# Attention in pairs of blocks from the eleventh on, and gate weights in fewer visits, in a kernel that fuses attention with two expert layers on one core

## The chip, the cores and the metric

The kernel runs on one core of a Trainium2 chip. The core has five engines, each with its own instruction stream that it follows in order: TensorE (PE in the rows; PEld is its loading of weights), VectorE (DVE), ScalarE (ACT), GpSimd (POOL) and SyncE (SP), which here issues DMA transfers. They meet at semaphores: an instruction that needs another engine's result waits at the head of its own stream, and whatever stands behind it waits too. The metric is the device time of one execution in microseconds.

## What is computed

```python
def _attn_ref(q, k, v):            # q, k, v: 4 batches, 8 heads, 576 positions, 64 values
    scores = scale * np.matmul(q, k.transpose(0, 1, 3, 2))
    ...                            # heads 0-3: a band of 32 keys; heads 4-7: 32 keys, four apart
    scores = np.where(masks[None], scores, -1000000000.0)
    scores = scores - np.max(scores, axis=-1, keepdims=True)
    attn = np.exp(scores)
    attn = attn / (np.sum(attn, axis=-1, keepdims=True) + 1e-09)
    return np.matmul(attn, v)

def _moe_ref(x, w1, w2, w3, w_out):  # x: 2304 tokens of 512; w1, w2: 512 x 1024; w3: 1024 x 1024
    a = x @ w1
    b = x @ w2
    h = a * b @ w3
    return h @ w_out

def _moe2_ref(x, w_gate, w1, w2):    # 8 experts, 288 tokens each, chosen by the gate's logits
    logits = x @ w_gate
    ...                              # tokens go to experts in the order of their logits
    out[mask] = np.maximum(x[mask] @ w1[e], 0.0) @ w2[e]
```

## The kernel before

**Attention** (L166 to L277) works on 36 blocks: 4 batches, each of 9 blocks of 64 query positions for all 8 heads; a key block has 96 keys. In each batch the ninth block (j = 8) holds what is left over, and its matmuls are cut into halves. A block goes through these steps: QK on TensorE (`att_qk`, L166, into two banks of PSUM); mask and row maximum on VectorE (`att_max`, L185); exponentials on ScalarE (`att_exp`, L197); the reciprocal of the sums on VectorE and the product of probabilities with it on GpSimd (`att_norm`, L203, L207); transposes on TensorE and a copy of them to SBUF on ScalarE (`att_tr`, L209, L213, L215); probabilities times V on TensorE (`att_av`, L217, L226 and L229); and the result's high half by a copy on ScalarE (L249, L250), its low half by a subtraction on VectorE (`att_out`, L232, L251, L252). PSUM has eight banks: four with the tag "ab", two "h", one "tr", one "rt". QK uses "h" from block 7 on, transposes "tr", V "rt".

`attention` (L254) is a generator that software-pipelines these: with each block t it issues QK of t, then, after a `yield`, the output of t - 4, the maximum of t and the norm of t - 1; after another `yield`, exponentials of t, transposes of t - 2 and V of t - 3; then QK of t + 1 follows in the same step. A step is what runs between two yields; a block has two steps. Each block so has **one visit** to TensorE: transposes of one block, V of another, QK of a third.

**The first expert layer** (`moe`, L397) multiplies x by w1 and w2 and the two results with each other. fp32 values are split into a high and a low part, so each product takes three matmuls (L433 to L435). `moe(b)` yields before every six matmuls of 512 columns (or twelve of 256); I call what stands between two of its yields a **portion**. Batch 0 has 32 portions: 16 on halves of 256 tokens, 16 on 512. Batches 1 and 2 have 32 too. Batch 3 has 48, 16 of them on all batches' ninth blocks. The accumulators are "ab" banks, taken out by a copy on ScalarE (L438) and a product on VectorE (L440) one portion later.

**The order** of everything is that in which the program text runs; no scheduler moves it. The main loop (L492 to L520) walks over the portions, and ahead of each runs steps of attention while `steps < done * ATT_RATE + ...` (L507; 0.65 steps per portion, and 0.7 more for each of batch 0's first eight), or for as long as the batch's input isn't ready: a portion of `moe(b)` must come behind the outputs of batch b that it reads, and a loop at a batch's end runs attention until these are issued. Ahead of each portion of batches 0 and 1 also runs one step of narrowing: weights come as 64-bit numbers and are turned into fp32 by three instructions on VectorE (L135, L137, L139), then split on ScalarE and GpSimd (L121, L124) in batch 0, or written back to DRAM (L314).

**The gates** (`gates`, L332): the second layer's gate is multiplied through w_out and w3 while batch 3's portions run. From its fourth portion on, each portion is preceded by one step: eight times transposes of a piece of w_out (`turn`, L341) and a product with the gate (`gate`, L352, L355), where each step has the product of one piece and the transposes of the next; then w3 in two groups of four (L369 to L378), where a step holds two of eight parts k (L376, 16 passes), and between the groups six portions pass while the second group is fetched.

Of the kernel before, what the change touches and what calls it, by code (L numbers as in the profile page):

```python
# [9 lines left out]
F32 = mybir.dt.float32  # L10
# [25 lines left out]
START, ATT_RATE, LATE, EARLY, FIRST = 8, 0.65, 3, 7, 0.7  # L36
# [51 lines left out]
def body(tc, qk_d, v_d, ke_d, ve_d, msk_d, cst_d, tri_d, w1_d, w2_d, w3_d, wo_d, wg_d, e1_d, e2_d, out):  # L88
# [12 lines left out]
    pa = pool("pa")  # L101
# [45 lines left out]
    QK, KE, SC, V, VE, P, OT, AV, X = {}, {}, {}, {}, {}, {}, {}, {}, {}  # L147
# [18 lines left out]
    def att_qk(t):  # L166
# [4 lines left out]
        s = SC[t] = [bank([128, 2, KB], "h" if t >= EARLY else "ab") for _ in range(2)]  # L171
# [13 lines left out]
    def att_max(t):  # L185
# [3 lines left out]
        p = pa.tile([128, 4, KB], F32, tag="p", name="p", bufs=3)  # L189
        sm = pa.tile([128, 4, 4], F32, tag="sm", name="sm", bufs=3)  # L190
# [18 lines left out]
    def att_tr(t):  # L209
        p = P.pop(t)[0]  # L210
        o = bank([KB, 4, 128], "tr" if t >= EARLY else "h")
        for i in range(4):
            nc.tensor.transpose(o[:, i, :], p[:, i, :], ident)  # L213
        pt = OT[t] = pa.tile([KB, 4, 128], F32, tag="pt", name="pt", bufs=2)
        act(pt, o, AF.Copy)  # L215

    def att_av(t):  # L217
        pt, v, ve = OT.pop(t), V.pop(t), VE.pop(t, None)
        o = AV[t] = bank([128, 4, QB], "rt")
# [34 lines left out]
    def attention():  # L254

        for t in range(NT + 4):
            if t < NT:
                att_qk(t)
            if t + 3 < NT:
                qk_load(t + 3)  # L260
            yield t - 4
            if t >= 4:
                att_out(t - 4)
            if t < NT:
                att_max(t)
            if 1 <= t <= NT:
                att_norm(t - 1)
            yield t - 3
            if t < NT:
                att_exp(t)  # L270
            if 2 <= t < NT + 2:
                att_tr(t - 2)
            if 3 <= t < NT + 3:
                att_av(t - 3)
            if t + 1 < NT:
                v_load(t + 1)

# [56 lines left out]
    def gates():  # L334
# [6 lines left out]
        def turn(r):  # L341
            g, i = divmod(r, 4)
            t = bank([128, 4, 128], "tr")
# [4 lines left out]
            wt = p3.tile([128, 4, 128], F32, tag="wt", name="wt", bufs=1)  # L348
# [8 lines left out]
        for r in range(8):  # L357
            wt = turn(r)
            yield
            gate(r, wt)  # L360
        ts = p3.tile([128, 4, 128], F32, tag="ts", name="ts", bufs=1)[:, :2]
# [10 lines left out]
        for a, ms in enumerate(((4, 5, 6, 7), (0, 1, 2, 3))):  # L372
            ws = [narrowed["w3", m] for m in ms]
            for k in range(8):
# [3 lines left out]
                if k % 2:  # L378
                    yield
# [4 lines left out]
        wt = p3.tile([128, 4, 128], F32, tag="wt", name="wt", bufs=1)[:, :2]  # L384
# [789 lines left out]
```

## Time and profile before

| | |
|---|---|
| time of three runs, us | 741.73 (median), 739.2, 743.91 |
| time of the profiled execution, us | 737.08 |
| its span, first to last instruction, us | 735.3 |
| TensorE busy, us (share) | 706.5 (96%) |
| weight loads busy | 609.8 (83%) |
| VectorE busy | 411.8 (56%) |
| ScalarE busy | 353.5 (48%) |
| GpSimd busy | 262.2 (36%) |
| granted TensorE clock, mean | 0.998 of 2.4 GHz |

Attention and the first layer's batches 0 to 2 fill the span to about 225 us, batch 3 with the gates to about 300 us; then come the product of w3 and w_out, the routing and the eight experts. A busy share of TensorE is made of overlapping matmuls whose ends are modelled, so the distance from one start to the next tells more than the duration. In the rows of the timeline the columns are start, duration, engine, line, operation, output from inputs, shape and how many instructions the row merges.

### The profile page before, as it was taken

The numbers are of one execution on the slowest core, as the hardware profiler recorded it, in microseconds if no ns is written. First come the engines' busy times: TensorE is split into PE (matmuls) and PEld (weight loads), VectorE is DVE, ScalarE is ACT, GpSimd is POOL, SyncE is SP. The second block draws the span as 40 slices with busy tenths as digits, with TensorE's granted clock in tenths as the row PEclk, the third lists the DMA queues.
The fourth block names the chain that finished last, engine by engine and source line by source line (L and its number), as shares of the span: only waits on it lengthen the run. The fifth ranks groups of instructions, "written<-read, shape, count | busy, mean of one in ns | idle before, by whom it ended". The sixth has DMA issues, their size and how long they took to land.

```text
span 735.3 us, 16004 instructions
## 1 busy us (share of the span) xinstructions
PE 706.5 (96%) x6081; PEld 609.8 (83%) x6081; DVE 411.8 (56%) x1414; ACT 353.5 (48%) x812; POOL 262.2 (36%) x305
## 2 busy tenths in 40 slices
PE   4799999999999999999999999999999999999996
PEld 3589787787788878687877877789999999999995
DVE  3879887863321001167876677678777863234321
ACT  4676555455422222243445375436556656665432
POOL 1758522121100033633355453331314144754521
PEclk9999999999999999999999999999999999999999
DMA  8984899862023030110699999869898798995311
GB/s 298 341 267 142 299 300 328 284 235 75 29 85 145 2 115 1 49 45 30 115 133 131 175 150 221 139 206 229 201 268 219 194 259 234 267 317 172 126 33 33
DMA packets 59452, 126.66 MB, mean 172 GB/s; under 512 B 13680, under 2 KB 29168, under 8 KB 56816
## 3 DMA queue, kind: packets, MB, share of 16 engines
q1 hardware_dynamic: 27088, 89.46, 36.8%
q0 software_dynamic: 29696, 31.46, 25.6%
q10 hardware_dynamic: 2592, 4.72, 1.9%
q8 instruction: 48, 0.79, 0.5%
q14 instruction: 28, 0.23, 0.1%
HBM read 87.87 MB, written 15.73 MB: 141 GB/s over the span
## 4 chain that ended last, share of the span: by engine, by line
PE 77%; issue 6%; DVE 5%; ACT 4%; DMA 3%; POOL 3%; SPq 1%; POOLq 0%; ACTq 0%; DVEq 0%
PE ps_ab L433 10%; PE ps_ab L435 9%; PE ps_ab L434 9%; PE ps_ab L578 4%; PE ps_h L999 4%; PE ps_h L1000 3%; PE ps_h L1001 3%; PE ps_ab L1023 3%; PE ps_ab L580 3%; PE ps_ab L579 3%; PE ps_ab L1024 3%; PE ps_ab L1025 3%; PE ps_rt L226 2%; PE ps_rt L776 2%; PE ps_ab L547 2%
## 5 line engine op out<-in xcount | busy, mean ns | idle before, releaser
L207 POOL TENSOR_TENSOR p<-p,sm 128x384 f32<-128x384 f32 x36 | 41.6, 1157 | 125.9 <-ACT p L200 68.3
L1023 PE MATMUL ps_ab<-hh,w 128*128 128x288 f32 x248 | 75.8, 306 | 0.0
L1025 PE MATMUL ps_ab<-hh,w 128*128 128x288 f32 x248 | 73.1, 295 | 0.0
L1024 PE MATMUL ps_ab<-hl,w 128*128 128x288 f32 x248 | 73.0, 294 | 0.0
L463 POOL DMA_DIRECT2D wbl<-g x36 | 48.4, 1675 | 62.8 <-ACT wbl L461 53.8
L1011 ACT ACTIVATE hh<-ps_h 128x288 fp32r<-128x288 f32 x62 | 25.5, 412 | 87.6 <-PE ps_h L1001 87.5
L200 ACT ACTIVATE p<-p,sm 128x96 f32<-128x96 f32 x144 | 52.1, 363 | 28.4 <-DVE sm L193 28.3
L1012 DVE SCALAR_TENSOR_TENSOR hl<-ps_h,hh 128x288 fp32r<-128x288 f32 x62 | 28.2, 455 | 66.3 <-ACT hh L1011 66.2
L438 ACT ACTIVATE a<-ps_ab 128x512 f32<-128x512 f32 (+1 forms) x44 | 22.8, 519 | 84.9 <-PE ps_ab L435 75.3
L578 PE MATMUL ps_ab<-Wx,wbh 128*128 128x512 f32 x144 | 59.7, 415 | 0.0
L579 PE MATMUL ps_ab<-Wx,wbh 128*128 128x512 f32 x144 | 56.3, 391 | 0.0
L580 PE MATMUL ps_ab<-Wx,wbl 128*128 128x512 f32 x144 | 56.2, 390 | 0.0
L433 PE MATMUL ps_ab<-x,wah 128*128 128x512 f32 (+1 forms) x144 | 55.9, 388 | 0.0
L440 DVE TENSOR_TENSOR g<-a,ps_ab 128x512 f32<-128x512 f32 (+1 forms) x36 | 22.4, 622 | 58.4 <-PE ps_ab L435 58.4
L433 PE MATMUL ps_ab<-x,wbh 128*128 128x512 f32 (+1 forms) x144 | 54.5, 379 | 0.0
L434 PE MATMUL ps_ab<-x,wah 128*128 128x512 f32 (+1 forms) x144 | 53.4, 371 | 0.0
L435 PE MATMUL ps_ab<-x,wal 128*128 128x512 f32 (+1 forms) x144 | 53.4, 371 | 0.0
L435 PE MATMUL ps_ab<-x,wbl 128*128 128x512 f32 (+1 forms) x144 | 52.8, 367 | 0.0
L434 PE MATMUL ps_ab<-x,wbh 128*128 128x512 f32 (+1 forms) x144 | 52.7, 366 | 0.0
L1024 PEld LDWEIGHTS ps_ab<-hl,w 128*128 128x128 f32 x248 | 46.7, 188 | 0.1
L1023 PEld LDWEIGHTS ps_ab<-hh,w 128*128 128x128 f32 x248 | 46.8, 189 | 0.0
L1025 PEld LDWEIGHTS ps_ab<-hh,w 128*128 128x128 f32 x248 | 46.5, 188 | 0.0
(293 smaller groups left out, 2052.9 us busy)
## 6 DMA issues: line engine op xcount, KB each, us to landing
est<-e_dram SPq DMA_DIRECT2D x53, 512.0 KB, 5.4
w<-w_dram SPq DMA_DIRECT2D x16, 1024.0 KB, 9.3
qk<-qk_dram SPq DMA_DIRECT2D x36, 320.0 KB, 5.3
w<-est POOLq DMA_DIRECT2D x20, 512.0 KB, 7.0
wbl<-g POOLq DMA_DIRECT2D x28, 256.0 KB, 6.3
v<-v_dram SPq DMA_DIRECT2D x36, 192.0 KB, 4.3
kept<-f SPq DMA_DIRECT2D x12, 512.0 KB, 4.9
rows<-e_dram SPq DMA_DIRECT2D x11, 512.0 KB, 6.3
```

The lines of the kernel that those rows point to most:

```text
L200: act(p[:, i, :], p[:, i, :], AF.Exp, bias=sm[:, 1, i:i + 1], scale=-1.0, accum_out=sm[:, 2, i:i + 1])
L207: nc.gpsimd.tensor_tensor(p, p, sm[:, 3, :, None].to_broadcast([128, 4, KB]), op=OP.mult)
L433: mm(a, wh[:, k, fs], xh[:, k, ts], start=(k == 0), stop=False)
L434: mm(a, wh[:, k, fs], xl[:, k, ts], start=False, stop=False)
L435: mm(a, wl[:, k, fs], xh[:, k, ts], start=False, stop=(k == 3))
L463: nc.gpsimd.dma_start(x, src, accum_op=OP.add)
L578: mm(a, h[:, f, :], wh, start=(f == 0), stop=False)
L579: mm(a, h[:, f, :], wl, start=False, stop=False)
L580: mm(a, l[:, f, :], wh, start=False, stop=(f == 7))
L1023: mm(y, wh[:, f % 2, ds_], h, start=(f == 0), stop=False)
L1024: mm(y, wh[:, f % 2, ds_], l, start=False, stop=False)
L1025: mm(y, wl[:, f % 2, ds_], h, start=False, stop=(f == end))
```

## The change

Up to block 9 attention runs as before. From block 10 on (`ALONE`) it goes two blocks at a time, in four steps per pair, and each stage has a visit to itself per pair: V of the pair `turned` (both into one "rt" bank), transposes of the pair `ready` (one into "tr", one into an "ab" bank), QK of the pair `new` (both into the two "h" banks), all in one step; then the copies of the transposes and the outputs of `turned`; then the first maximum and both norms of `scored`; then the second maximum and both exponentials. A pair's QK is so three visits ahead of its V. The probability buffers become four, and the rate of steps in batch 0 is 0.72 (`RUSH`) in place of 0.65. In the gates, two pieces of w_out are turned per two steps, in "h" banks and with two buffers, and w3 takes one step per group of four.

```diff
-START, ATT_RATE, LATE, EARLY, FIRST = 8, 0.65, 3, 7, 0.7
+START, ATT_RATE, RUSH, LATE, EARLY, FIRST, ALONE = 8, 0.65, 0.72, 3, 7, 0.7, 10
...
     ident = C[:, C_ID:C_ID + 128]
-    QK, KE, SC, V, VE, P, OT, AV, X = {}, {}, {}, {}, {}, {}, {}, {}, {}
+    QK, KE, SC, V, VE, P, TR, OT, AV, X = {}, {}, {}, {}, {}, {}, {}, {}, {}, {}
...
-    def att_qk(t):
+    def att_qk(t, s=None):
         x = QK.pop(t)
-        s = SC[t] = [bank([128, 2, KB], "h" if t >= EARLY else "ab") for _ in range(2)]
+        s = SC[t] = s or [bank([128, 2, KB], "h" if t >= EARLY else "ab") for _ in range(2)]
         ke = KE.pop(t, None)
...
         m = 2 if j == 8 else int(j < 4)
-        p = pa.tile([128, 4, KB], F32, tag="p", name="p", bufs=3)
-        sm = pa.tile([128, 4, 4], F32, tag="sm", name="sm", bufs=3)
+        p = pa.tile([128, 4, KB], F32, tag="p", name="p", bufs=4)
+        sm = pa.tile([128, 4, 4], F32, tag="sm", name="sm", bufs=4)
         for i in range(4):
...
-    def att_tr(t):
+    def att_tr(t, tag):
         p = P.pop(t)[0]
-        o = bank([KB, 4, 128], "tr" if t >= EARLY else "h")
+        o = TR[t] = bank([KB, 4, 128], tag)
         for i in range(4):
             nc.tensor.transpose(o[:, i, :], p[:, i, :], ident)
+
+    def att_pt(t):
         pt = OT[t] = pa.tile([KB, 4, 128], F32, tag="pt", name="pt", bufs=2)
-        act(pt, o, AF.Copy)
-
-    def att_av(t):
+        act(pt, TR.pop(t), AF.Copy)
+
+    def att_av(t, o=None):
         pt, v, ve = OT.pop(t), V.pop(t), VE.pop(t, None)
-        o = AV[t] = bank([128, 4, QB], "rt")
+        o = AV[t] = bank([128, 4, QB], "rt") if o is None else o
         for i in range(4):
...
-        for t in range(NT + 4):
-            if t < NT:
-                att_qk(t)
-            if t + 3 < NT:
-                qk_load(t + 3)
+        for t in range(ALONE):
+            att_qk(t)
+            qk_load(t + 3)
             yield t - 4
                 att_out(t - 4)
-            if t < NT:
-                att_max(t)
-            if 1 <= t <= NT:
+            att_max(t)
+            if t:
                 att_norm(t - 1)
             yield t - 3
-            if t < NT:
-                att_exp(t)
-            if 2 <= t < NT + 2:
-                att_tr(t - 2)
-            if 3 <= t < NT + 3:
+            att_exp(t)
+            if t >= 2:
+                att_tr(t - 2, "tr" if t - 2 >= EARLY else "h")
+                att_pt(t - 2)
+            if t >= 3:
                 att_av(t - 3)
-            if t + 1 < NT:
-                v_load(t + 1)
-
+            v_load(t + 1)
+        att_out(ALONE - 4)
+        turned, ready, scored, done = [ALONE - 3], [ALONE - 2], [ALONE - 1], ALONE - 3
+        qk_load(ALONE + 3)
+        t = ALONE
+        while done < NT:
+            new = list(range(t, min(t + 2, NT)))
+            t += 2
+            if turned:
+                o = bank([128, len(turned), 4, QB], "rt")
+                for i, x in enumerate(turned):
+                    att_av(x, o[:, i])
+            for x, tag in zip(ready, ("tr", "ab")):
+                att_tr(x, tag)
+            if new:
+                o = [bank([128, 2, 2, KB], "h") for _ in range(2)]
+                for i, x in enumerate(new):
+                    att_qk(x, [y[:, i] for y in o])
+                for x in (t + 2, t + 3):
+                    if x < NT:
+                        qk_load(x)
+            yield done
+            for x in ready:
+                att_pt(x)
+            for x in turned:
+                att_out(x)
+                done = x + 1
+            for x in scored:
+                if x not in V:
+                    v_load(x)
+            yield done
+            for x in new[:1]:
+                att_max(x)
+            for x in scored:
+                att_norm(x)
+            yield done
+            for x in new[1:]:
+                att_max(x)
+            for x in new:
+                att_exp(x)
+            yield done
+            turned, ready, scored = ready, scored, new
...
             g, i = divmod(r, 4)
-            t = bank([128, 4, 128], "tr")
+            t = bank([128, 4, 128], "h")
             for q in range(4):
                 nc.tensor.transpose(t[:, q, :], w[:, n0:n0 + 128], ident)
-            wt = p3.tile([128, 4, 128], F32, tag="wt", name="wt", bufs=1)
+            wt = p3.tile([128, 4, 128], F32, tag="wt", name="wt", bufs=2)
             act(wt, t, AF.Copy)
...
-        for r in range(8):
-            wt = turn(r)
+        for r in range(0, 8, 2):
+            wts = [turn(r), turn(r + 1)]
             yield
-            gate(r, wt)
-        ts = p3.tile([128, 4, 128], F32, tag="ts", name="ts", bufs=1)[:, :2]
+            yield
+            for i in range(2):
+                gate(r + i, wts[i])
+        ts = p3.tile([128, 4, 128], F32, tag="wt", name="ts", bufs=2)[:, :2]
         act(ts, acc, AF.Copy)
...
                        start=(k == 0), stop=(k == 7))
-                if k % 2:
-                    yield
+            yield
             if ms[0]:
                     yield
-        wt = p3.tile([128, 4, 128], F32, tag="wt", name="wt", bufs=1)[:, :2]
+        wt = p3.tile([128, 4, 128], F32, tag="wt", name="wt", bufs=2)[:, :2]
         act(wt, acc, AF.Copy)
...
             while b < 3 and nxt is not None and nxt < NB * (b + 2) and (
-                    steps < done * ATT_RATE + (min(done, 8) * FIRST if b == 0 else 0) or nxt < NB * b + (8 if part else 4)):
+                    steps < done * (RUSH if b == 0 else ATT_RATE) + (min(done, 8) * FIRST if b == 0 else 0) or nxt < NB * b + (8 if part else 4)):
                 nxt = next(att, None)
```

**What this does to TensorE's order.** Around portion 3, at the join of the two schemes, TensorE had a visit of transposes of block 7 (L213), V of block 6 (L226) and QK of block 10 (L179), as it has one for every block:

```order
L213 MATMUL ps_tr<-C,p 96x128 x4
L226 MATMUL ps_rt<-pt,v 64x64 x8
L179 MATMUL ps_h<-qk 64x96 x8
L433 MATMUL ps_ab<-x,wbh 128x256
L434 MATMUL ps_ab<-x,wbh 128x256
```

In the changed program (whose line numbers are a little higher: L228 is V, L472 the first matmul of a portion) that visit reads:

```order
L213 MATMUL ps_tr<-C,p 96x128 x4
L228 MATMUL ps_rt<-pt,v 64x64 x16
L213 MATMUL ps_tr<-C,p 96x128 x4
L179 MATMUL ps_h<-qk 64x96 x16
L472 MATMUL ps_ab<-x,wbh 128x256
```

V of blocks 6 and 7 stand behind each other, 8 matmuls each, then transposes of block 8 and QK of blocks 10 and 11. Later visits in the changed program, here the one after portion 15 of batch 0 (the tags `ps_tr` and `ps_ab` are the two banks of a pair's transposes), have this order, with 18 to 48 large matmuls to the next:

```order
L228 MATMUL ps_rt<-pt,v 64x64 x16
L213 MATMUL ps_tr<-C,p 96x128 x4
L213 MATMUL ps_ab<-C,p 96x128 x4
L179 MATMUL ps_h<-qk 64x96 x12
L182 MATMUL ps_h<-qk 32x96
```

V comes first now, then the transposes of two blocks, then QK of two (here the second is a ninth block). The visits stand after portions 1, 2, 3, 6, 9, 15, 21, 26 and 32 of batch 0.

On GpSimd, in batch 0, the products of probabilities (L207) alternated with the splits of weights (L124):

```order
L207 TENSOR_TENSOR p<-p,sm 128x384 x2
L124 TENSOR_TENSOR wal<-f,wah 128x256 x4
L207 TENSOR_TENSOR p<-p,sm 128x384 x2
L124 TENSOR_TENSOR wbl<-f,wbh 128x256 x4
L207 TENSOR_TENSOR p<-p,sm 128x384
```

At the same place the changed program has:

```order
L207 TENSOR_TENSOR p<-p,sm 128x384
L124 TENSOR_TENSOR wal<-f,wah 128x256 x4
L207 TENSOR_TENSOR p<-p,sm 128x384 x2
L124 TENSOR_TENSOR wbl<-f,wbh 128x256 x4
L207 TENSOR_TENSOR p<-p,sm 128x384 x2
```

Products that were asked for in different steps and happened to be neighbours are now asked for in pairs, in one step; the pair in the middle is that of blocks 10 and 11.

## Rows read from the trace of the kernel before

**Rows 1.** The page's busy times: engine, us, share, instructions.

```profile
PE 706.5 (96%) x6081; PEld 609.8 (83%) x6081; DVE 411.8 (56%) x1414; ACT 353.5 (48%) x812; POOL 262.2 (36%) x305
```

**Rows 2.** TensorE's waits, 38 to 300 us: total us, times, longest.

```profile
PE ps_rt L226 <- PE ps_tr L213: 1.2, 2, 1.0
```

**Rows 3.** One stretch: length, busy us of PE, PEld, DVE, ACT, POOL; clock; DMA.

```profile
50.00:75.00 25.00, 23.69 (x283) 21.74 (x282) 22.56 (x73) 16.19 (x56) 18.17 (x17) 1.00 0.51 158
```

**Rows 4.** Timeline of TensorE: one visit in the steady part.

```profile
118.06 0.39 PE L435 MATMUL ps_ab<-x,wbl 128*128 128x512 f32 x1
118.29 0.60 PE L213 MATMUL ps_tr<-C,p 128*96 128x128 f32 x4
118.82 0.69 PE L226 MATMUL ps_rt<-pt,v 96*64 96x64 f32 x16
119.43 0.56 PE L179 MATMUL ps_h<-qk 64*64 64x96 f32 x16
119.92 0.50 PE L433 MATMUL ps_ab<-x,wbh 128*128 128x512 f32 x1
120.26 0.40 PE L434 MATMUL ps_ab<-x,wbh 128*128 128x512 f32 x1
120.49 0.40 PE L435 MATMUL ps_ab<-x,wbl 128*128 128x512 f32 x1
```

**Rows 5.** Timeline of TensorE: V, then QK, of a ninth block.

```profile
106.81 0.45 PE L226 MATMUL ps_rt<-pt,v 96*64 96x64 f32 x8
...
107.68 0.56 PE L179 MATMUL ps_h<-qk 64*64 64x96 f32 x16
...
137.05 0.40 PE L179 MATMUL ps_h<-qk 64*64 64x96 f32 x8
...
137.70 0.50 PE L433 MATMUL ps_ab<-x,wah 128*128 128x512 f32 x1
```

**Rows 6.** Timeline of TensorE: the last block's V, behind a large matmul.

```profile
213.84 0.39 PE L435 MATMUL ps_ab<-x,wal 128*128 128x512 f32 x1
214.16 0.45 PE L226 MATMUL ps_rt<-pt,v 96*64 96x64 f32 x8
```

**Rows 7.** Timeline of TensorE: transposes for the gates; product and transposes.

```profile
229.00 0.60 PE L347 MATMUL ps_tr<-C,wo 128*128 128x128 f32 x4
229.36 0.36 PE L433 MATMUL ps_ab<-xt,wbh 128*128 128x256 f32 x1
...
230.97 0.42 PE L355 MATMUL ps_rt<-wt,wg 128*32 128x128 f32 x8
...
231.74 0.36 PE L433 MATMUL ps_ab<-xt,wah 128*128 128x256 f32 x1
```

**Rows 8.** Timeline of TensorE: one visit of w3.

```profile
250.96 0.28 PE L435 MATMUL ps_ab<-xt,wal 128*128 128x256 f32 x1
...
251.30 0.28 PE L376 MATMUL ps_rt<-S,TS 128*32 128x128 f32 x2
...
251.52 0.28 PE L376 MATMUL ps_rt<-S,TS 128*32 128x128 f32 x2
...
251.74 0.39 PE L433 MATMUL ps_ab<-xt,wbh 128*128 128x256 f32 x1
251.96 0.28 PE L434 MATMUL ps_ab<-xt,wbh 128*128 128x256 f32 x1
```

**Rows 9.** Timeline around block 6's V: TensorE, ScalarE, VectorE [idle before <- releaser].

```profile
43.15 0.69 PE L226 MATMUL ps_rt<-pt,v 96*64 96x64 f32 x16
...
44.44 0.58 ACT L215 ACTIVATE pt<-ps_tr 96x512 f32<-96x512 f32 x1
...
46.29 0.39 ACT L250 ACTIVATE x<-ps_rt 128x128 fp32r<-128x128 f32 x1
...
46.71 0.29 DVE L251 TENSOR_TENSOR x<-ps_rt,x 128x128 fp32r<-128x128 f32 x1 [2.32 <-ACT x L250]
```

**Rows 10.** GpSimd's products, 36 to 126 us (min/median/max ns); narrowing on VectorE.

```profile
L207 POOL TENSOR_TENSOR p<-p,sm x16: 816/1111/1820, 39.2 to 121.9; 128x384 f32<-128x384 f32 x16
...
L137 DVE SCALAR_TENSOR_TENSOR f<-w,f 128x1024 int32<-128x1024 int32 x11 | 16.9, 1534 | 0.2
```

## The prediction

> **What bounds the kernel now.** I read the page first. TensorE is busy for 706.5 of the span's 735.3 us [rows 1]. A busy share says little by itself (pipelined matmuls overlap in it), so the list of waits came next: between 38 and 300 us, where both edits lie, TensorE waited twice, 1.2 us in all [rows 2]. The table of stretches shows it busy for 23.7 of the 25 us from 50 on, with VectorE close behind, 22.6 [rows 3]. So in this stretch the time is TensorE's instruction stream, and a saving there counts unless it turns into a wait; VectorE is the engine that could make one.
>
> Then the timeline, for what the stream spends on attention. In the steady part one visit to attention stands between two large matmuls: four transposes, 16 passes of probabilities times V, 16 of Q times K (a trace shows two passes per fp32 matmul), from 118.29 to 119.92 us, 1.63 us; the first large matmul after it takes 0.34 us to the next start, the second 0.23 [rows 4]. There are 32 such visits from the first portion (six matmuls of 512 columns, or twelve of 256; 1.4 us) to the last block: 28 with all three parts, three with two, one with one.
>
> How much of a visit is work and how much is changing from one shape of matmul to another? Blocks with j = 8 have 24 passes, not 16. V then takes 0.87 us, not 0.61, so 16 passes are worth 0.52 and 0.09 is fixed; QK takes 0.65, not 0.49, so 0.32 is work and 0.17 fixed [rows 4, 5]. Four full transposes between matmuls of their own shape cost 0.36 [rows 7]; the attention ones, followed by V, cost 0.53: 0.17 fixed. With 0.11 on the first large matmul, a visit has 0.54 us that does not grow with its work. Where V follows a large matmul without a transpose, that matmul's step is 0.32, so this entry costs 0.09 [rows 6].
>
> **Attention in pairs, the saving.** Before: 28 x 0.54, three visits at 0.37 (transposes, V, back) and one at 0.29, 16.5 us in all. After, by the order of TensorE's instructions, 19 visits: two unpaired, one transitional (transpose, V twice, transpose, QK), 13 in the order V, transposes, QK, two of V and transposes, one of V. A pair's visit has entry 0.09, V's own 0.09, transposes to QK 0.17, QK to large 0.11, and one change that no row has: V to transposes. It is bounded by nothing (transposes into the large matmul cost nothing [rows 7]) and by 0.26 (transposes to V, both sides); I take 0.17, the middle of the three changes that rows show. That makes 0.63 per pair against 1.08. The 13 cost 8.2, the other six 2.8 (0.54 twice, 0.71, 0.35 twice, 0.29), 11.0 in all: **5.5 us saved**, 8.2 if the new change is free, 4.1 at 0.26.
>
> The Trainium skill says, in "TensorEngine Tiling (Array Packing)", Key Properties, that changing the tiling mode, not just the tile, drains TensorE. By that the new order buys a fourth drain per visit, which speaks against it; the sum by that rule is the one with 0.17 to 0.26, 5.5 to 4.1 saved. The rows agree that a change of shape costs and that transposes beside full-array matmuls do not.
>
> **Gates and w3.** A w3 visit of 16 passes runs from 251.08 (250.96 and a step of 0.12) to 251.74, and the first large matmul takes 0.22, not 0.12; its sets of four are 0.11 apart, 0.44 of work, so 0.32 is fixed [rows 8]. Eight visits become two: 6 x 0.32 = 1.9 us. A gate visit with its transposes takes 0.77, with 0.09 of entry; less 0.36 for the transposes and 0.22 for two sets of four, 0.28 is fixed [rows 7]. Eight become four: 1.1 us. TensorE is at its bound there and waits for nothing [rows 2], so **3.0 us** come off the path. The transposed tiles get a second buffer and the two "h" banks, which batch 3 leaves idle; the wait for w3's second half still has its six portions. These moves I cost at nothing; they are covered by the portions between a copy and its use, 2.8 us, and without that cover each would cost the 0.6 us of a copy.
>
> **New waits.** First, the join. After block 6's V the same step issues V for block 7. Both use the one "rt" bank, so the second waits until ScalarE and VectorE have taken the first out. Before, a portion lay between. In the trace block 6's V starts at 43.15; ScalarE is in an exponential, then copies the transposed probabilities until 45.02 [rows 9]; two copies of the result follow (0.55 for both, estimated from 0.39 of the second), then two subtractions (0.6, from 0.29 of the first), to 46.1, against 43.8 without a wait: **2.3 us**. Queued behind it are the transposes and both QK, and after those all matmuls. Bounds: 1.2 if ScalarE is free, 3.5 as at 46.71, where the subtraction came that long after V began.
>
> Second, the visit after portion 9 transposes blocks 10 and 11 one portion after their two products are asked of GpSimd in one step, behind VectorE's narrowing. Before, one product was asked at a time, with more than a portion between. A product takes 1.11 us in the median [rows 10]. If VectorE reaches both norms when asked, 2.2 us of products stand against 1.43 of portion and 0.6 of V, about nothing; if a narrowing instruction (1.53) and the second row maximum come first, up to 3.1. VectorE has 2.4 idle us in 25 here [rows 3], so nearer late: **1.9 us**.
>
> Third, batch 1 begins right behind the forced visit that issues V of block 16, whose result it reads. The visit ends 3.0 us after that V begins. V and transposes take 2.0, then two copies of transposed probabilities end at 2.6, result copies 3.15, subtraction 3.75: **0.8 us**, from nothing up to 2.3, what VectorE once waited for such copies [rows 9]. Before, the result was ready ahead of time.
>
> Given back: the 1.2 us of listed waits [rows 2], whose cause, V one visit after its transposes in a crowded ScalarE queue, is relaxed. SyncE's queue: each visit now issues two QK loads together, after both QK; their use is two visits away. V loads find their buffer free. The next weight load stands behind them about 4 us later, and its narrowing is needed eight portions on: nothing. The fourth probability buffer is needed so that two blocks are in work; nothing by itself. The higher RUSH rate moves VectorE work earlier within batch 0, which is in the second wait.
>
> **Sum:** -5.5 - 3.0 + 2.3 + 1.9 + 0.8 - 1.2 = **-4.7 us**. The profiled execution's span is 735.3, its reported time 737.08; the sum gives 730.6 and 732.4. That execution is 0.6% below the median of the three shown, 741.73, so against the median I predict **737.0 us**.
>
> **Rivals.** (1) No new waits: VectorE and ScalarE, less interleaved, have each result ready. For it: VectorE idles 2.32 us at 46.71 for ScalarE's copies [rows 9], and pairs take that ring apart. Against: the join is in the instruction order whatever the queues do. -9.7, 732.0 us; with a free fourth change 729.3.
>
> (2) Slower: the two products back to back become TensorE's wait in all of batch 0, not once. There are four more pair visits in it after the one counted; at the upper price of 3.1 each, and the first raised by 1.2, it adds 13.6: 750.6. It decides from about 12 us of such waits on. For it: VectorE at 90%, products up to 1.82 us [rows 10]. Against: from 38 us on no listed wait is for a product [rows 2], and after portion 9 the visits are 5 to 6 portions apart, 7 to 8 us, against 2.2 of products.
>
> The Trainium skill bears on this one: "GPSIMD Engine Reference", 1. Specifications, has GpSimd's SBUF interfaces shared with VectorE, in contention when VectorE runs a two-port mode or has two SBUF inputs. By that rule each product beside narrowing takes 1.82, and the second wait is 1.4 us longer: 738.4, or this rival if it recurs. The spread from 0.82 to 1.82 us agrees; which one a pair gets, no row here shows.
>
> (3) The saving doesn't come: 0.54 us belongs to a block, not to a visit (each block's 16 passes start in a fresh accumulator). Then -3.0 + 5.0 - 1.2 = +0.8, 742.5. Against: the first large matmul's 0.11 and the entry can't belong to a block.
>
> **How the numbers follow.** Forecast 0.58, (1) 0.27, (2) 0.08, (3) 0.07. The forecast's own range is 734.5 to 741: waits at their lower bounds or a cheap fourth change, against the upper bounds of the three waits and 4.1 saved. The range given, 731 to 743, takes in (1) and (3) and leaves out (2) and the free fourth change. One per cent, 7.4 us, is about what a measurement of this kernel can tell from no change. Faster by over that is most of (1) and an edge of the forecast, 0.30; slower is (2), 0.07; within 1% the rest, 0.63.
>
> **What would show it.** Right: pair visits of about 3.0 us in the steady part and two w3 visits of about 2; 19 attention visits; a step near 2.3 us between V of blocks 6 and 7; gaps at the transposes after portion 9 and at batch 1's first matmuls. Wrong: a pair visit of 3.2 or more without a wait (3); no gap at the ninth portion (1); listed waits of TensorE for GpSimd's p in several visits (2); or a change in the stages after 330 us, which I count at nothing because their instructions are unchanged.

## The result, and the profile after

The changed kernel takes **744.17 us** in the median of 20 runs (741.68 to 748.53), the kernel before 739.97 beside it (737.23 to 746.3): a ratio of **1.0053**, interval 1.0037 to 1.0069. It is slower by half a per cent, where 737.0 was forecast and 743 was the top of the range. (A ratio here and below is between kernels timed in turn on one chip; a median runs over all runs of a kernel, so the two need not agree to the last us.) The profiled execution of after has a span of 745.9 us, reported as 747.71, which is 3.5 above its median; 735.3 was that of before.

The page first: busy engines, and the granted clock in 40 slices of 18.6 us.

```profile
PE 705.3 (95%) x6081; PEld 614.7 (82%) x6081; DVE 408.6 (55%) x1414; ACT 352.8 (47%) x812; POOL 264.4 (35%) x305
...
PEclk9699989999999999999999999979999999999998
```

The 6 in the second slice lies ahead of the first visit that the change reorders, and three profiles of the experiments have it too, one of them of the kernel before with an edit that acts later. TensorE's busy time hardly differs from [rows 1], so the page doesn't show the loss. The list of TensorE's waits between 38 and 300 us does, beside 1.2 us in [rows 2] (line, what released it, total us, times, longest):

```profile
PE ps_tr L213 <- POOL p L207: 4.3, 2, 4.0
PE ps_rt L228 <- DVE x L254: 2.9, 1, 2.9
PE ps_ab L213 <- POOL p L207: 1.9, 2, 1.1
PE ps_rt L228 <- ACT wbh L121: 1.6, 1, 1.6
```

Of these 10.7 us, 3.0 are waits that the prediction names: 1.6 at the join, 0.3 + 1.1 behind portion 9. The other 7.7 stand in one place, behind portion 21, in the visit that does V of blocks 12 and 13. TensorE's timeline there, from the last matmul of a portion (start, us, what; in brackets idle time and its releaser):

```profile
84.03 0.39 PE L474 MATMUL ps_ab<-x,wal 128*128 128x512 f32 x1
87.32 1.15 PE L228 MATMUL ps_rt<-pt,v 96*64 96x64 f32 x32 [2.90 <-DVE x L254]
92.46 1.09 PE L213 MATMUL ps_tr<-C,p 128*96 128x128 f32 x4 [3.99 <-POOL p L207]
94.31 1.09 PE L213 MATMUL ps_ab<-C,p 128*96 128x128 f32 x4 [0.76 <-POOL p L207]
...
96.81 0.79 PE L472 MATMUL ps_ab<-x,wah 128*128 128x512 f32 x1
97.41 0.63 PE L473 MATMUL ps_ab<-x,wah 128*128 128x512 f32 x1
```

From its V to the next large matmul this visit takes 9.50 us; its like later (126.03 to 128.94, below) takes 2.91. V waits for VectorE's output of block 11, the transposes for GpSimd's products, and those for VectorE's reciprocals. So all three waits lead to VectorE:

```profile
73.33 0.41 DVE L479 TENSOR_TENSOR g<-a,ps_ab 128x256 f32<-128x256 f32 x1
84.87 0.69 DVE L135 TENSOR_SCALAR f<-w 128x1024 int32<-128x1024 int32 x1 [11.13 <-DMA w<-wo_dram]
85.48 0.28 DVE L253 TENSOR_TENSOR x<-ps_rt,x 128x128 fp32r<-128x128 f32 x1
...
86.89 0.37 DVE L254 TENSOR_TENSOR x<-ps_rt,x 128x128 fp32r<-128x128 f32 x1
...
90.95 0.18 DVE L206 RECIPROCAL sm<-sm 128x4 f32<-128x4 f32 x1
```

VectorE stands for 11.13 us at the first narrowing of w_out, with both outputs, the maxima and the reciprocals queued behind it. GpSimd, whose next work hangs on them, is idle for as long:

```profile
91.03 3.22 POOL L207 TENSOR_TENSOR p<-p,sm 128x384 f32<-128x384 f32 x2 [12.18 <-DVE sm L205]
```

And w_out is late because of SyncE. Its timeline:

```profile
75.53 0.97 SPq L154 DMA_DIRECT2D qk<-qk_dram  x2
76.60 1.21 SPq L128 DMA_DIRECT2D w<-wo_dram  x2
```

and the longest of what its queue waited for between 40 and 130 us (total, times, longest):

```profile
SPq L154 <- PE ps_h L179: 45.2, 9, 8.6
```

In the kernel before that list begins with loads of V, and none of its rows is a QK load:

```profile
SPq L161 <- PE ps_rt L226: 34.5, 13, 4.1
```

Its first two loads of w_out:

```profile
69.83 4.18 SPq L128 DMA_DIRECT2D w<-wo_dram  x2
```

QK has four buffers, and a load three blocks ahead takes the buffer of the block behind the current one, long read. A pair's two loads, four blocks ahead of the blocks just issued, take the buffers of those very blocks: SyncE stands at them until TensorE has run this QK (74.91 to 75.89). Behind them in the queue, from the step of portion 15, come the first two loads of w_out, 6.8 us later than before; and VectorE had reached their first use at 73.74. The chain of waits goes that way (start, us, what):

```profile
76.08 0.41 SPq L154
76.60 8.18 DMA w<-wo_dram
84.93 0.55 issue
```

Last, the stretches around the wait: length, busy us of PE, PEld, DVE, ACT, POOL, then the granted clock and the DMA's share.

```profile
75.00:85.00 10.00, 9.41 (x82) 7.62 (x82) 0.13 (x1) 1.19 (x4) 3.85 (x6) 1.00 0.80 274
85.00:90.00 5.00, 1.15 (x32) 1.01 (x32) 4.37 (x11) 1.16 (x3) 0.00 (x0) 0.97 0.28 85
90.00:95.00 5.00, 1.78 (x8) 1.28 (x8) 4.90 (x23) 3.68 (x17) 3.22 (x2) 0.50 0.86 300
95.00:100.00 5.00, 5.00 (x42) 3.77 (x41) 3.69 (x18) 1.78 (x6) 0.00 (x0) 0.50 0.50 103
100.00:105.00 5.00, 5.00 (x24) 4.11 (x22) 4.36 (x13) 2.93 (x15) 3.67 (x2) 1.00 0.98 388
```

VectorE, 22.6 us busy of 25 in [rows 3], does 0.13 in ten. And after TensorE has worked 1.15 of 5 us, its clock stands at half (1.2 GHz) until 100: large matmuls 0.43 us apart, not 0.23.

### The profile page after: what moved, and what is told of

It reads as the page before. It is cut to its first block, busy times and chain, and to the rows that moved or that the text cites. A ratio compares the mean times of both kernels' runs of the same rounds, so it can differ in the third digit from the quotient of the medians.

```text
span 745.9 us, 15939 instructions
## 1 busy us (share of the span) xinstructions
PE 705.3 (95%) x6081; PEld 614.7 (82%) x6081; DVE 408.6 (55%) x1414; ACT 352.8 (47%) x812; POOL 264.4 (35%) x305
## 4 chain that ended last, share of the span: by engine, by line
PE 75%; DVE 7%; issue 6%; DMA 4%; POOL 3%; ACT 3%; SPq 1%; POOLq 0%; DVEq 0%; ACTq 0%
PE ps_ab L472 9%; PE ps_ab L473 8%; PE ps_ab L474 8%; PE ps_ab L617 4%; PE ps_ab L618 3%; PE ps_ab L619 3%; PE ps_h L1038 3%; PE ps_h L1039 3%; PE ps_h L1040 3%; PE ps_ab L1062 3%; PE ps_ab L1064 3%; PE ps_ab L1063 3%; PE ps_rt L815 2%; PE ps_rt L228 2%; PE ps_ab L586 2%
## 5 line engine op out<-in xcount | busy, mean ns | idle before, releaser
L207 POOL TENSOR_TENSOR p<-p,sm 128x384 f32<-128x384 f32 x36 | 45.8, 1286 | 125.8 <-DVE sm L205 100.0
L472 PE MATMUL ps_ab<-x,wah 128*128 128x512 f32 (+1 forms) x144 | 55.0, 382 | 0.1
L472 PE MATMUL ps_ab<-x,wbh 128*128 128x512 f32 (+1 forms) x144 | 54.1, 376 | 0.0
```

What stands on the lines that cost most here:

```text
L207: nc.gpsimd.tensor_tensor(p, p, sm[:, 3, :, None].to_broadcast([128, 4, KB]), op=OP.mult)
L472: mm(a, wh[:, k, fs], xh[:, k, ts], start=(k == 0), stop=False)
```

## The experiments

Beside each ratio stands, from its one profile, the **stretch** from the visit behind portion 3 to the first matmul of the logits. It takes in the first visit that the change reorders and all later attention and gates: 262.9 us before (42.62 to 305.54), 266.9 after (43.81 to 310.68).

**The w_out loads early.** The first narrowing issues them.

```diff
             get12(j + 4)
+            if j >= 6:
+                get3(j - 6)
...
-        get3(0)
-        get3(1)
         for j in range(12):
```

> The changed kernel, with one difference: the first two loads of the second narrowing (w_out, 1 MB each) are issued as soon as their buffers come free, one three portions earlier and so ahead of the two QK loads of the visit after portion 15, not behind them. Theory A (the loads' place in SyncE's queue): VectorE's wait of 11.1 us for the load falls to 1 us or less, the visit after portion 21 falls from 9.5 us plus 3.1 ahead of it to about 2.9, the half-clock stretch at 90 us goes, and the time falls by about 10 us, to 0.99 of the kernel before or a little under (the stage up to the gate's logits ends at 300 us in place of 310.7). Theory B (VectorE is simply overloaded by pairs in batch 0): VectorE is late at the same place whatever the loads do, and the time stays within 3 us of the changed kernel's, 1.005 of before.

736.62 us, ratio 0.9948 (0.9923 to 0.9973), stretch 257.5. SyncE issues the first load at 69.85, ahead of the pair's QK loads:

```profile
69.85 0.35 SPq L128 DMA_DIRECT2D w<-wo_dram  x1
77.43 0.88 SPq L154 DMA_DIRECT2D qk<-qk_dram  x2
```

and the stretch around the former stall reads (columns as above):

```profile
85.00:100.00 15.00, 14.94 (x182) 11.94 (x181) 11.61 (x41) 8.01 (x37) 5.19 (x4) 1.00 0.98 331
```

TensorE's wait and the half clock are gone. VectorE still waits 2.1 us for w_out at the longest (3.3 in all, where at most 1 was expected), without TensorE waiting behind it. The changed kernel without the stall is faster than the one before.

**Gates alone, pairs alone.** The kernel before with the changed `gates` function; and the changed kernel with the old one.

```diff
-        for r in range(8):
-            wt = turn(r)
+        for r in range(0, 8, 2):
+            wts = [turn(r), turn(r + 1)]
             yield
-            gate(r, wt)
+            yield
+            for i in range(2):
+                gate(r + i, wts[i])
...
-                if k % 2:
-                    yield
+            yield
```

The second kernel has the same lines with + and - changed about.

> The kernel before with the changed gates alone. By the prediction's step 3.0 us less than before (ratio 0.996); by the traces of both kernels, visits of the gates and w3 with their entries 2.8 us less. Rival: the tensors' later or earlier place moves something behind it (the split of w3 and w_out that is paced by the same portions), and the gain does not reach the end: 1.000.

> The changed kernel with the gates as before: pairs alone. If the two parts add, 3 us slower than the changed kernel, 1.009 of before, with the same 11 us wait of VectorE for the w_out load and the same visit of 9.5 us after portion 21. If the gates' part gave nothing, 1.005.

Gates alone: 736.66 us, 0.9966 (0.9945 to 0.9987), stretch 258.7. Pairs alone: 749.56, 1.012 (1.0077 to 1.0162), stretch 272.3, with the stall (VectorE waits 10.4 us for w_out, TensorE's clock is 0.68 from 85 to 100 us). The 1.009 expected for pairs alone lies within its interval. So the loss belongs to the pairs.

**The old rate.**

```diff
-START, ATT_RATE, RUSH, ... = 8, 0.65, 0.72, ...
+START, ATT_RATE, RUSH, ... = 8, 0.65, 0.65, ...
```

> The changed kernel with batch 0's rate of attention back at 0.65 steps a portion. The visits of batch 0 move to later portions, so the w_out loads, which are asked for at portion 15, stand ahead of a pair's QK loads. Theory A: VectorE's wait for the load falls below 2 us and the 9.7 us at portion 21 go; but at the end of batch 0 more steps are forced in a row (two visits without portions between), which costs 3 to 6 us at batch 1's start. In all 0.990 to 0.998 of before. Theory B: VectorE is late as before but less so, 1.00 to 1.005, with the wait for products still in several visits.

738.69 us, 0.9974 (0.9944 to 1.0005), stretch 261.7. The pair of blocks 16 and 17 moves behind portion 17, its loads behind those of w_out (68.54); VectorE's longest wait for w_out is 0.9 us. Whether a pair and the narrowing start in one step is enough to decide the stall. What its going is worth, this run doesn't show: V at the join waits 2.6 us here, transposes wait 1.5 for a product at 109.22, the granted clock is 0.83 from 40 to 60 us and 0.91 from 100 to 120, and the stretch is only 1.2 shorter than before.

**Loads late, VectorE not standing at them.** Nothing changes on SyncE up to these loads, but five portions pass between the loads and their use.

```diff
         get3(0)
         get3(1)
+        for _ in range(5):
+            yield
         for j in range(12):
```

> The changed kernel with one edit: the second narrowing issues its first two w_out loads where it did, behind the pair's QK loads in SyncE's queue, and then lets five portions go by before VectorE takes the first of them. The loads land as late as in the changed kernel; only VectorE no longer stands at them with its outputs, maxima and reciprocals queued behind. Theory (the 9.7 us come from VectorE standing at the head of its queue for a load that SyncE issued late): VectorE's wait for w_out falls from 11.1 us to under 2, TensorE's waits in portion 15 and in the visit behind it (3.3 and 7.6 us) go, ratio to the kernel before 0.995 (736 us; 734 to 739), as with the loads issued early. Rival (the loads themselves, or the visit of blocks 16 and 17, are slow whoever waits for them): TensorE still waits 5 us and more there, ratio 1.00 to 1.005.

(TensorE's 3.3 us named there stand at the end of portion 21, not in portion 15.) 738.65 us, 0.9952 (0.9925 to 0.9979), stretch 258.1. The loads are as late as in after, and VectorE still waits at them, but the outputs and reciprocals of these blocks are no longer behind:

```profile
78.48 1.21 SPq L128 DMA_DIRECT2D w<-wo_dram  x2
...
86.62 0.69 DVE L135 TENSOR_SCALAR f<-w 128x1024 int32<-128x1024 int32 x1 [4.44 <-DMA w<-wo_dram]
```

TensorE is busy throughout:

```profile
85.00:100.00 15.00, 15.00 (x184) 12.15 (x184) 10.69 (x32) 8.03 (x33) 3.13 (x2) 1.00 0.74 243
```

VectorE's wait is longer than expected (under 2 us; 6.5 in its two waits for w_out) and costs TensorE nothing. What counts is what stands behind the load in VectorE's queue, not that the load is late.

**QK loads late.** The other end of SyncE's queue: a pair's QK loads are issued in the pair's last step, when their buffers have been read.

```diff
-                for x in (t + 2, t + 3):
-                    if x < NT:
-                        qk_load(x)
...
             for x in new:
                 att_exp(x)
+            if new:
+                for x in (t + 2, t + 3):
+                    if x < NT:
+                        qk_load(x)
             yield done
```

> The changed kernel with one edit at the other end of SyncE's queue: a pair's QK loads are issued in the pair's last step, not right behind its QK products, so that SyncE doesn't stand at a QK buffer when the second narrowing issues its w_out loads. Theory (SyncE's queue order alone): VectorE waits under 2 us for w_out, ratio 0.995 (736.5 us; 734 to 739) as with the early loads, though the narrowing's place is unchanged. The QK loads land some three portions later and are still ahead of the next pair's QK by more than the 2 to 4 us that such a load takes. Rival (portion 15's narrowing is late for its own reason, the w_out transfer of 1 MB each): VectorE still waits 8 us or more, ratio 1.00 to 1.005.

733.67 us, **0.9897** (0.9863 to 0.9931), stretch 256.3. The narrowing is where it was, and w_out's first load goes out at 67.36, the second by 73.2:

```profile
63.20 1.98 SPq L154 DMA_DIRECT2D qk<-qk_dram  x2
67.36 5.81 SPq L128 DMA_DIRECT2D w<-wo_dram  x2
```

VectorE waits 1.0 us for w_out in all. Faster than expected; that it beats the early loads is within their two intervals.

**Early loads in the kernel before.** The edit of the first experiment, alone: the control.

> The kernel before with one edit: the second narrowing's first two w_out loads issued early, from the first narrowing, as in the run that mended the changed kernel. In the kernel before they land in time but for 1.2 us on VectorE, and TensorE waits for nothing behind them. Theory (the early loads give back only what the changed order lost): no change, ratio 1.000 (0.997 to 1.003), 740 us. Rival (early loads are worth something by themselves, to any kernel, so that the gain of the mended kernels isn't the stall's): 736 to 737, ratio 0.995.

739.25 us, 0.9979 (0.9952 to 1.0005), stretch 261.6. No change that can be told: by the interval, early loads alone are worth half a per cent at most. The stretch also shows what two profiles of nearly the same work differ by, 1.3 us.

**Transposes first.** Early loads, and the transposes ahead of V in a pair's visit.

```diff
+            for x, tag in zip(ready, ("tr", "ab")):
+                att_tr(x, tag)
             if turned:
                 o = bank([128, len(turned), 4, QB], "rt")
                 for i, x in enumerate(turned):
                     att_av(x, o[:, i])
-            for x, tag in zip(ready, ("tr", "ab")):
-                att_tr(x, tag)
```

> The changed kernel with the two w_out loads issued early (736.6 us, ratio 0.995) and one more edit: in a visit of a pair the transposes stand ahead of the V products, so the order is portion, transposes, V, QK instead of portion, V, transposes, QK. A visit then has three changes between full-array and half-array tiles instead of four. If the change from V to transposes costs what entering a visit from a portion costs (0.09 us) to what V behind a portion costs (0.26 us), the 16 pair visits and the join give 1.5 to 4 us back: 733 to 735 us, ratio 0.990 to 0.993. Rival: the change between V and transposes costs nothing, or V waits for the transposes' copies instead: 736.6 us, ratio 0.995, and the steady visit stays at 2.91 us.

736.47 us, 0.9952 (0.9927 to 0.9978), stretch 257.7, no gain. Its steady visit:

```profile
139.54 0.39 PE L474 MATMUL ps_ab<-x,wbl 128*128 128x512 f32 x1
139.77 0.60 PE L213 MATMUL ps_tr<-C,p 128*96 128x128 f32 x4
...
140.74 1.15 PE L228 MATMUL ps_rt<-pt,v 96*64 96x64 f32 x32
...
142.64 0.50 PE L472 MATMUL ps_ab<-x,wah 128*128 128x512 f32 x1
```

and the longest of its listed waits:

```profile
PE ps_ab L213 <- POOL p L207: 2.5, 3, 1.1
PE ps_tr L213 <- POOL p L207: 1.2, 2, 0.8
```

From the last matmul to the visit's end are 3.10 us, in after 3.23 (below): 0.13 a visit, some 2 us in all, as expected. But the transposes, 1.1 us sooner, wait 3.7 us for products and not 1.1 as with the early loads alone, and that takes it back.

**An early join; products earlier; both.** An empty step ahead of the first pair (with early loads); the norms of `scored` one step earlier (with late QK loads); both (with late QK loads).

```diff
         t = ALONE
+        yield done
...
                     v_load(x)
+                att_norm(x)
             yield done
             for x in new[:1]:
                 att_max(x)
-            for x in scored:
-                att_norm(x)
```

> The changed kernel with the two w_out loads issued early (736.6 us, ratio 0.995) and one more edit: a step without work between the blocks that go alone and the first pair, so that the V products of block 7 no longer follow those of block 6 in one visit. Theory (the join's wait at the V bank, 1.6 to 1.7 us, goes with the time that the step gives the two narrowed outputs of block 6): the wait goes from the rows, 735 us, ratio 0.9925. Rival: block 7's V waits for something else as long (its own transposes' copy, or the products on GpSimd), or the step's extra visit costs as much: 736.6 us, ratio 0.995.

> The changed kernel with the pair's QK loads issued in its last step (733.7 us, ratio 0.990) and the reciprocals and GpSimd products of a pair one step (a portion) earlier, the join as it is. Theory: the 1.4 us that transposes wait for products falls to nothing, 732.3 us, ratio 0.988. Rival: the products are late because GpSimd is behind with low halves, not because of their place; then the wait stays at 1 us or more and the time at 733.7.

> The changed kernel with the pair's QK loads issued in its last step (733.7 us, ratio 0.990) and two more edits: the empty step ahead of the first pair, and the reciprocals and GpSimd products of a pair one step earlier. What is left of TensorE's waits in the first 330 us is 1.5 us for V behind the join and 1.4 us for transposes behind GpSimd's products; if both edits take theirs away and nothing takes their place: 731 us, ratio 0.987. Rival: the two savings don't come, since the norm's reciprocals now wait on VectorE for the exponentials and hold up the maxima, and the join's step only moves its wait: 733.7 us, ratio 0.990, with a new wait for maxima or outputs in the rows.

Early join: 736.31 us, 0.9926 (0.9894 to 0.9958), stretch 256.9; products: 732.92, 0.9905 (0.9867 to 0.9943), 255.7; both: 735.56, 0.9922 (0.9892 to 0.9952), 258.6. The early join's wait for the bank goes, and so does the products' 1.4 us with the earlier products and with both; with both, though, V at the join still waits 0.95 us. And others come. In the order of the three kernels, V behind the join, the first matmul of batch 1, and a QK behind portion 22:

```profile
46.38 0.69 PE L228 MATMUL ps_rt<-pt,v 96*64 96x64 f32 x16 [0.97 <-DMA v<-v_dram]
```

```profile
109.48 0.49 PE L472 MATMUL ps_ab<-x,wah 128*128 128x512 f32 x1 [1.04 <-ACT x L251]
```

```profile
85.93 1.72 PE L179 MATMUL ps_h<-qk 64*64 64x96 f32 x32 [1.44 <-issue]
```

None of the three shows a gain over its base outside the intervals, so they don't tell theories from rivals by time: the early join's ratio is its theory's (0.9925), its time the rival's; the earlier products lie between theirs (732.3 and 733.7 us); with both edits the theory's 0.987 is out. In each a new wait of 1.0 to 1.4 us stands in the rows.

**Late QK loads at the old rate.**

> The changed kernel with the pair's QK loads issued in its last step (733.7 us, ratio 0.990) and with the old rate 0.65 in batch 0 as well (RUSH 0.65). This tells the two parts apart that the run with the old rate alone mixed: without the stall the rate only spreads the pairs. Theory: the order on SyncE was the whole loss of the changed kernel, so the rate is worth little by itself: 733 to 736 us, ratio 0.989 to 0.994. Rival: the faster rate saves waits at the batch's end (block 8 before batch 1's first QK): 737 to 739, ratio 0.996 to 0.998.

738.38 us, 0.9958 (0.9936 to 0.998), stretch 256.8. The time lies in the rival's range (737 to 739), not in the theory's (733 to 736). But the stretch is only 0.6 us longer than at 0.72, while the median is 4.7 us higher; in the two profiles 1.1 us of the difference lie ahead of the stretch and 1.1 behind the logits, where no edit is. What the rate is worth stays open.

## Why the prediction was wrong, step by step

**The step that failed is SyncE's queue**, put as "V loads find their buffer free. The next weight load stands behind them about 4 us later, and its narrowing is needed eight portions on: nothing." Three things in it are wrong. The QK loads themselves don't find their buffers free (SyncE waits 45.2 us for QK, 8.6 at most), and V loads wait too, if less (7.3 us in two waits). The weight load behind them wasn't 4 but 6.8 us later than before. And I asked when the narrowed weight is needed, not what is queued behind the narrowing on VectorE: an instruction in an in-order queue is needed as soon as the next one behind it is. The narrowing's first step stands ahead of the outputs of 10 and 11 and the reciprocals of 14 and 15, which TensorE needs within a visit. The rows of order that I had laid out were TensorE's and GpSimd's; SyncE's would have shown the loads behind the pair's.

Its size: 7.7 us of listed waits. The visit takes 6.59 more than its like, 4.75 of it waits, so 1.84 are slower matmuls, nearly all in transposes and QK from 92 us on; the seven large steps from 96.81 to 99.97 take 3.16 against 1.72 (0.34 and six of 0.23), 1.44 more. That is 11.0 us. Between the visits behind portions 15 and 32 lie 43.79 us in after (72.81 to 116.60) and 32.77 with the loads late but VectorE free (74.76 to 107.53): 11.0. With the early loads (74.72 to 107.88) and with the late QK loads (72.22 to 105.42) they are 33.2 long: 10.6.

**Attention's saving, 5.5, was about 5.0, of two errors against each other.** A steady visit of after, 32 passes of V and of QK:

```profile
125.71 0.39 PE L474 MATMUL ps_ab<-x,wbl 128*128 128x512 f32 x1
126.03 1.15 PE L228 MATMUL ps_rt<-pt,v 96*64 96x64 f32 x32
127.11 0.64 PE L213 MATMUL ps_tr<-C,p 128*96 128x128 f32 x4
...
128.12 0.89 PE L179 MATMUL ps_h<-qk 64*64 64x96 f32 x32
128.94 0.50 PE L472 MATMUL ps_ab<-x,wah 128*128 128x512 f32 x1
129.28 0.39 PE L473 MATMUL ps_ab<-x,wah 128*128 128x512 f32 x1
```

With the entry's 0.09 and the first large step's 0.11 it takes 3.11; the work of two blocks by the prediction's prices is 2.40, so 0.71 is fixed, not 0.63. The one unknown, V to transposes, is then 0.25: its upper bound, not the middle that I took. It stands in 15 visits (12 with V, transposes and QK, two without QK, and the join): 1.2 less saved. But the visits are 18, not 19: 26 blocks make 13 pairs, and the first pair's QK is in the transitional visit, so 12 are left where the prediction counts 13. The one too many was priced at 0.63, which is saved on top: 11.5 fixed in all, not 11.0 (nor 12.2, as 19 visits would give), against 16.5 before. That two wrong terms come out near 5.5 is luck. The Trainium skill ("TensorEngine Tiling (Array Packing)", Key Properties) has a drain at each change of mode; here the trace agrees, in that the fourth change costs its 0.25.

**Gates and w3, 3.0, were right**: the gates alone give 0.34% (0.13 to 0.55), 2.5 us (1.0 to 4.1). A visit of after has 16 passes and eight transposes in 1.42 us:

```profile
241.13 0.64 PE L393 MATMUL ps_rt<-wt,wg 128*32 128x128 f32 x16
...
242.55 0.36 PE L472 MATMUL ps_ab<-xt,wbh 128*128 128x256 f32 x1
```

against two visits of 0.77 with eight and four [rows 7]. With entry and the first large step that is 1.59 against two of 0.94; the two w3 visits are 2.07 each against four of 0.77. All visits of gates and w3 together take 3.2 us less. Nothing waits for the moved copies.

**The new waits** were where the prediction put them, and a little smaller. V of block 7, then the transposes of 10 and 11:

```profile
44.34 0.69 PE L228 MATMUL ps_rt<-pt,v 96*64 96x64 f32 x16
46.61 0.69 PE L228 MATMUL ps_rt<-pt,v 96*64 96x64 f32 x16 [1.58 <-ACT wbh L121]
...
60.82 0.64 PE L213 MATMUL ps_tr<-C,p 128*96 128x128 f32 x4 [0.26 <-POOL p L207]
62.60 0.64 PE L213 MATMUL ps_ab<-C,p 128*96 128x128 f32 x4 [1.14 <-POOL p L207]
```

The join costs 1.7 us (46.61 less 44.34 and 0.61 of V) for 2.3; the row names a copy of weights, but VectorE's subtraction from the bank ends at 46.35, which is what V needs. The products cost 1.4 for 1.9. Batch 1's first matmul starts 1.03 after its visit's QK (118.94 to 119.97; 0.82 in a steady visit), and its step takes 0.61 (to 120.58), 0.3 more than in [rows 4]: 0.5 in all, for 0.8; in the run with earlier products it waits 1.04. The old waits of [rows 2] are gone, as said.

**The sum without the stall** is then -5.0 - 3.2 + 1.7 + 1.4 + 0.5 - 1.2 = -5.8, for -4.7. The stretch without it is shorter than before by 5.4 (early loads), 4.8 (VectorE free) and 6.7 (late QK loads), and the three ratios give 3.6 to 7.6 us. After's stretch is 8.8 to 10.6 longer than theirs. With the stall's 11.0 that makes +5.2; the stretch is 4.0 longer in after's profile, the median 4.2, and two profiles of like work differed by 1.3. The forecast's mechanism and most sizes hold; one queue, costed at nothing, turned the sign.

**The rivals.** (2), slower through the products, had the right sign and the wrong place: TensorE's longest wait is for a product, but the product waits for VectorE, once, not for GpSimd in every visit. (1), no new waits, and (3), no saving, are out by the rows above. That (3)'s time, 742.5, came nearest to the measured one is luck.

The profiled execution of after takes 5.5 us more behind the logits (435.2 for 429.8), where I count nothing: among others its clock falls again behind a wait of 1.63 us for gathered rows (488.75) and is 0.53 from 490 to 500. The profiles differ there though no edit is there: 433.8 in the kernel before with the early loads, 436.7 with the gates alone, both with a clock of 0.83 from 480 to 500. And the medians, 4.2 us apart, leave no room for it; it isn't the change's cost as such.

## What to carry to other kernels

When two loads are issued ahead instead of one, count the buffers: with as many blocks in flight as buffers, the load waits for the reader just issued, and all that its queue holds behind it waits too. Price a late instruction by what stands behind it on its own engine, not by when its result is used; then either issue the load from a step where its buffer is free, or leave room between a load's issue and the place where an engine takes it. Late QK loads alone make the changed kernel 1% faster than the one before (0.9897), with earlier products the same (0.9905), and either beats both kernels.

## What the runs showed of the hardware

A wait costs more than its length: in both kernels with the stall TensorE's clock was at half from about 90 to 100 us (0.66 and 0.68 over 85 to 100), and 3.3 of the 11.0 us are matmuls at that clock. In the kernel before and in all kernels without the stall it is 1.00 over that stretch, but for one (0.89), in which TensorE waits 1.44 us for a QK there (85.93, above). Half clocks of a few us come elsewhere too: from 30 to 45 us the clock is 1.00 in the kernel before and 0.74 in it with the early loads, 0.72 in after and 0.74 in after with the early loads. What else sets them off stays open.

SyncE's order mattered more than its rate: two loads of w_out, 1 MB each, went out together, and the first was ready for use 8.18 us after its issue. The Trainium skill ("Trainium Kernel Development and Optimization", Quick Reference, Key Constraints) has it that issuing DMAs from several engines only saves the sequencer's issue time. Here an issue of about 0.4 us stood at its buffer for up to 8.6, and the loads behind it with it; the rows put that wait beside the issue time which the rule counts. Loads from another queue weren't tried, so no run here tests the rule.

GpSimd's two products behind portion 9 took 2.61 us together, the first under 0.9 (begun at 59.94; its transposes start at 60.82), the second, in part beside VectorE's two-input narrowing (60.64 to 61.86), about 1.7. The Trainium skill ("GPSIMD Engine Reference", 1. Specifications) has the two contend in that case, and the trace agrees for this one pair; no run takes the narrowing away from it.
